# Attention scores on four quadrants of the matrix array, one chunk's router logits by VectorE, and a new step order, in a fused attention, MLP and routed-expert kernel

## The chip, the cores and the metric

The kernel runs on one core of one Trainium2 chip. The metric is the device time of one execution in microseconds (us). A core has five engines with a queue each: TensorE (PE: matmuls, and PEld: the weight loads before them), VectorE (DVE), ScalarE (ACT), GpSimd (POOL) and SyncE (SP, which issues most DMAs). Matmuls write PSUM; the other engines read it and work in SBUF.

## What is computed

Three layers follow each other; `x` goes from one to the next.

```python
# 1: attention of 2 batches x 8 heads x 768 positions, head_dim 64
k_sum = k.reshape(B, H, nb, 32, D).max(axis=3)       # 24 blocks a head
v_sum = v.reshape(B, H, nb, 32, D).mean(axis=3)
scores_l = where(|i - j| < 16, q @ k.T / 8, -1e9)    # a narrow window
scores_s = q @ k_sum.T / 8 + log(32)                 # and every block
a = softmax(concat(scores_l, scores_s)); out = a @ concat(v, v_sum)
# 2: x of 1536 tokens x 512
h = x @ w_in                                         # 512 x 2048
x = (h * sigmoid(h)) @ w_out                         # 2048 x 512
# 3: the best of 8 experts for each token
e = argmax(x @ w_gate)                               # 512 x 8
out = gate * (relu(x @ w1[e]) @ w2[e])               # 512 x 1024, 1024 x 512
```

## The kernel before

**Chunks.** The 1536 tokens are 6 chunks of 256 (`CH`), three to a batch; a chunk is 4 query tiles of 64 (`G`, `QT`). Heads go in pairs (`HP` = 4), 64 rows of head dimension each, so that a pair fills 128 partitions. A query tile needs 96 window keys and the 24 block keys: 120 columns (`NC`).

**Attention of a chunk and a head pair** is a row of steps, each one function: `D` (`dots`, line 318, scores on PE), `T` (`lows`, mask and maximum on DVE), `E` (`exps`, ACT), `R` (`shares`, DVE), `N` (`norm`, DVE), `P` (`turn`, four transposes on PE), `C` (`keep`, a copy out of PSUM), `V` (`values`, line 378, PE), `H` and `L` (`x_high`, `x_rest`: the result split in a high and a low part for ACT and DVE). `q` loads: for chunks 0 and 1 the queries alone, later also windowed keys and values. The keys of chunks 0 and 1 are cut from whole key tiles (`k`, loaded; `K`, block maxima on DVE; `W`, `windows`, POOL). The host lays the queries of a pair out as a block diagonal: the tile has 128 rows (two heads) and 128 columns (64 queries of one head, 64 of the other), with zeros in the two other blocks. One fp32 product of 128x128 with 120 moving columns so gives the scores of both heads, and a step has four such products into one PSUM tile (pool `ps_x` for chunks 0 and 1, `ps_a` later).

**The MLP** runs on split operands (a high part and a rest, three products for each). `F` (line 403, 24 products of N=256, the first four blocks in parts F0 to F3) makes 256 columns of h for a chunk in one of two PSUM tiles of pool `ps_h`; `t` (tanh, ACT), `u` (gating, DVE, the last reader of h), `g` and `w` split the result; `G` (line 440, 12 products of N=512) adds it into the chunk's two `ps_x` tiles. Its weights arrive packed (`l`), and steps `a`, `b`, `c`, `h`, `p` on ACT and DVE unpack and split them during the first 120 us. `x` copies a finished chunk out.

**The router** has two ways. `d` (`route_dots`, line 475): 16 products of a row tile with a broadcast column of `w_gate`, summed by DVE. Or, for the chunks named in `TURNED`, (4, 5) here: `rt` (line 486, four transposes on PE a tile), `rc` (a copy), `rl` (line 498, products with the gate on PE). `i`, `r` and `e` pick the expert, rank the tokens and write the table. After chunk 4 an early plan (`plan`, `prow`) chooses the first two expert units; `read`, `ids` and `ga` gather their tokens, `f1` and `f2` fetch their weights at an address from a register that the plan writes, `1h`, `1r`, `2h`, `2r` split those, `lt` turns the tokens. Then `f` (line 825 or 819) and `z` (line 866 or 860) are the experts' two layers, `ym` and `yo` scale and write.

**The order** of all this work is one list, `STEPS`: each word calls the next instance of one step, and each engine's queue has its instructions in that order. A mark says which engine takes a copy (' DVE, * ACT, _ POOL).

Of the kernel before, what the change touches and what calls it, by code (L numbers as in the profile page):

```python
# [58 lines left out]
C0* C0* D1 D1 D1 T1 E1 T1 T1 E1 P0 q1 C0* v0 b V0 H0 l l v0 R1 R1 L0 c v1 E1 N1 A0_ a V0 H0 R1 v0 A0_ N1 N1 V0 L0 H0 L0 h* a p h* b D1 b p P1 C1* l a A1_ l P1 P1 C1*  # L59
C1* l c F0 A0_ v0 V0 v1 v1 c h* V1 F0 F0 T1 h' H0 L0 F0 p b p F1 E1 F1 R1 c A1_ A1_ H1 L1 a b t u V1 v1 a l H1 V1 F1 H1 a N1 A1_ F2 q2 q2 A2_ F1 t l L1 P1 C1* L1 F2  # L60
F2 l l l l A2_ l V1 c b b a u c D2 T2 h* h* H1 L1 p b c p F3 F3 F3 g* w g* w F3 D2 h* p F2 c E2 a b h* p c t u l a t u h* h* p p a a b b c c g* g* G G l l a a a F t
F t w G w R2 N2 P2 h* h* b b c l h* c h* b p p p u u p b G C2* V2 a F c g* w l l F X q2 a c b b T2 c l l h* h* g* w c p t E2 G G h* h' u p p p F t H2 u g' a a b w a
l b a c t R2 N2 h* l c h* L2 G A2* p l P2 l b c b u l D2 T2 g* w F p c C2* V2 E2 h* p G h' p q2 A2_ F g* w G a b a b a a c c t h' h* b b D2 u g* l l l l c F h* w G l
p p p t c h' p a a t u u g' b b c w c F g* F H2 L2 T2 h* h* p p a E2 j G R2 N2 P2 w b c G t C2* q3 V2 u h' p R2 N2 P2 g* a w G q3 b c h' p F F t H2 u g' w L2 j G a a
b c h' p t j b u g' t u j C2' c h' p V2 H2 m m m m w L2 J B3' F F F t u g* g' J J w D3 t u T3 B3* J E3 G G R3 w D3 G t s g' w s N3 P3 u x* G g* s T3 C3' F E3 R3 N3
P3 w O d0 q3 s t u B3_ q3 Y M A3* G q4 A3' V3 F d0 d0 d0 C3* V3 g' w d0 t d0 d0 d0 B3_ u H3 G L3 H3 L3 D3 D3 T3 E3 T3 E3 d0 g' w F t F R3 R3 N3 N3 d0 u g* w P3 C3' t
u q4 g* B4_ D4 G A3* V3 H3 P3 A3' C3* T4 F E4 G d0 d0 d0 R4 N4 L3 t u g' d0 d0 d0 V3 H3 L3 F B4_ i r e e t F t w w u g' u w D4 T4 E4 x' d1 d1 d1 G F t q4 d1 d1 d1
B4_ P4 D4 T4 E4 q4 R4 A4* C4' G G V4 N4 P4 C4' R4 u d1 d1 d1 d1 g' F g* B4_ N4 t F w w t u g' u g' H4 L4 w D4 T4 E4 G G P4 C4* A4_ V4 d1 H4 F t R4 d1 q5 d1 d1 A4_ V4
H4 N4 L4 u g* d1 F B5' D5 G A5' w d1 q5 x* B5_ L4 T5 E5 i P4 C4' D5 T5 E5 d2 A4_ w F V4 H4 R5 R5 d2 L4 G N5 P5 t u d2 d2 d2 g* w d2 t u g* F r q5 N5 d2 d2 t u d2 d2
d2 w d2 d2 G G g* F t u g' F w d2 t u d2 d2 B5' C5' q5 G x* g' F F t t i V5 H5 d3 d3 w w d3 d3 d3 d3 d3 d3 L5 P5 G G u g' u D5 C5' T5 E5 F R5 e e A5_ V5 d3 d3 N5 g'  # L70
# [24 lines left out]
def fused_kernel(ctx: ExitStack, tc, qw, kw, kt, vw, vr, vt, w_in, w_out, w_gate, w1, w2, masks, blocks, items, out):  # L95
# [180 lines left out]
    qs, ks, vs, ws, dot = {}, {}, {}, {}, {}  # L276
# [790 lines left out]
```

## Time and profile before

| | before |
|---|---|
| median of 3 runs | 541.26 us (540.97 to 544.36) |
| the profiled execution | 540.3 us |
| its span, first to last instruction | 538.4 us |
| PE, DVE, ACT, POOL busy | 520.3, 427.4, 227.6, 81.5 us |
| moved by DMA | 76.25 MB |

The profile is one execution. The span leaves out 1.9 us around the instructions. An engine's busy time is the union of its instructions; matmuls are pipelined, so that what one costs is read from the distance between starts, or from a run of them on the chain that ended last, and not from its duration. A transfer costs when someone waits for it.

### The profile page before, as it was taken

What the parts mean: (1) busy time and instruction counts of PE and PEld (TensorE: products, weight loads), DVE (VectorE), ACT (ScalarE), POOL (GpSimd) and SP (SyncE); (2) the same over time, 40 slices, a digit from 0 to 9 for tenths busy, and PEclk for the clock granted to TensorE, in tenths of its full rate; (3) what the DMA queues carried; (4) which work ended last, traced back from release to release, by engine and by line L of the source; (5) the groups of instructions that cost most, each with busy time, mean ns of one, the idle gap of its engine ahead of it and who ended that gap; (6) DMA issues with size and microseconds to landing.
All of it is one profiled execution on the core that took longest, in us unless ns stands there. A gap on an engine that the chain in (4) does not pass through costs nothing.

```text
span 538.4 us, 9847 instructions
## 1 busy us (share of the span) xinstructions
PE 520.3 (97%) x3602; PEld 458.7 (85%) x3602; DVE 427.4 (79%) x1114; ACT 227.6 (42%) x546; POOL 81.5 (15%) x113
## 2 busy tenths in 40 slices
PE   7779999999999999999999999999999999999993
PEld 4579888989889898898988989898989889988882
DVE  4899999997778797788886364968769786879991
ACT  3799987652324332341122312242423422344551
POOL 3711000100000021001010323010334210220041
PEclk9999999999999999999999999999999999999997
DMA  8998545326573311420200208300264750347950
GB/s 326 367 311 304 178 158 167 97 84 211 175 243 97 92 54 54 126 73 5 88 16 1 40 1 313 110 9 1 62 241 141 265 196 0 106 163 266 326 187 15
DMA packets 40936, 76.25 MB, mean 142 GB/s; under 512 B 3910, under 2 KB 14764, under 8 KB 40882
## 3 DMA queue, kind: packets, MB, share of 16 engines
q1 hardware_dynamic: 35954, 65.83, 36.3%
q0 software_dynamic: 2912, 6.33, 3.3%
q10 hardware_dynamic: 2016, 3.40, 2.0%
q8 instruction: 30, 0.49, 0.4%
q14 instruction: 24, 0.20, 0.1%
HBM read 82.51 MB, written 7.19 MB: 167 GB/s over the span
## 4 chain that ended last, share of the span: by engine, by line
PE 79%; issue 11%; DVE 3%; ACT 2%; POOL 2%; DMA 1%; POOLq 0%; DVEq 0%; ACTq 0%
PE x L440 25%; PE h L403 25%; PE jh L825 11%; PE jy L866 9%; PE s L326 3%; PE o L384 2%; POOL out L875 2%; PE t L366 2%; ACT a L351 1%; PE xp L793 1%; DMA kt<-kt 1%; PE lo L504 1%; DVE dull L481 0%; DVE a L360 0%; DVE ksum L184 0%
## 5 line engine op out<-in xcount | busy, mean ns | idle before, releaser
L403 PE MATMUL h<-x,wi 128*128 128x256 f32 x1152 | 144.7, 282 | 0.0
L440 PE MATMUL x<-wo,g 128*128 128x512 f32 x576 | 142.5, 399 | 0.1
L403 PEld LDWEIGHTS h<-x,wi 128*128 128x128 f32 x1152 | 139.0, 188 | 1.8 <-DVE wi L270 0.2
L440 PEld LDWEIGHTS x<-wo,g 128*128 128x128 f32 x576 | 105.5, 188 | 23.5 <-DVE g L424 0.4
L786 DVE TENSOR_TENSOR sp<-r,sp 128x512 fp32r<-128x512 f32 x144 | 92.0, 683 | 7.7 <-ACT sp L164 7.3
L825 PE MATMUL jh<-xTT,sp 128*128 128x256 f32 x576 | 73.7, 284 | 0.0
L825 PEld LDWEIGHTS jh<-xTT,sp 128*128 128x128 f32 x576 | 71.6, 191 | 1.5
L866 PE MATMUL jy<-sp,jT 128*128 128x512 f32 x288 | 70.8, 397 | 0.0
L866 PEld LDWEIGHTS jy<-sp,jT 128*128 128x128 f32 x288 | 52.8, 188 | 11.4
L164 ACT CAST sp<-r 128x512 fp32r<-128x512 f32 x74 | 42.6, 620 | 42.3 <-DMA r<-w 30.1
L413 ACT ACTIVATE t<-h 128x512 f32<-128x512 f32 x48 | 28.5, 596 | 61.7 <-PE h L403 34.2
L351 ACT ACTIVATE a<-a,m 128x120 f32<-128x120 f32 x96 | 36.7, 384 | 36.0 <-DVE m L345 35.9
L416 DVE SCALAR_TENSOR_TENSOR t<-t,h 128x512 f32<-128x512 f32 x48 | 32.6, 682 | 16.4 <-ACT t L413 16.0
L481 DVE CUSTOM_DVE_ANT_0 dull<-row,gate 128x512 bf16<-128x512 f32 x64 | 44.1, 690 | 1.3
L834 ACT ACTIVATE jT<-jh 128x512 fp32r<-128x512 f32 x24 | 14.4, 598 | 58.9 <-PE jh L825 42.0
L424 DVE TENSOR_TENSOR g<-t,g 128x512 fp32r<-128x512 f32 x48 | 32.9, 695 | 3.5 <-ACT g L164 3.2
L164 DVE CAST sp<-r 128x512 fp32r<-128x512 f32 x70 | 28.3, 424 | 8.7 <-PE jh L825 6.4
L875 POOL DMA_INDIRECT out<-y,ids x15 | 21.3, 1419 | 74.3 <-ACT y L871 50.4
L164 POOL COPY k<-ksum 128x96 f32<-128x96 f32 x11 | 4.0, 363 | 176.2 <-DMA k<-kw 166.7
L345 DVE CUSTOM_DVE_ANT_0 a<-s,mask 128x120 f32<-128x120 f32 x96 | 21.2, 277 | 10.6 <-PE s L326 9.3
L164 ACT CAST g<-t 128x512 fp32r<-128x512 f32 x27 | 16.6, 622 | 26.6 <-DVE t L416 26.2
L552 POOL DMA_INDIRECT tbl<-tb,ix x12 | 12.7, 1056 | 63.1 <-DVE cum L544 60.8
(185 smaller groups left out, 618.9 us busy)
## 6 DMA issues: line engine op xcount, KB each, us to landing
r<-w SPq DMA_DIRECT2D x36, 1024.0 KB, 5.6
rawi<-w_in SPq DMA_DIRECT2D x16, 512.0 KB, 5.5
rawo<-w_out SPq DMA_DIRECT2D x16, 512.0 KB, 7.8
q<-qw SPq DMA_DIRECT2D x24, 256.0 KB, 6.9
v<-vw SPq DMA_DIRECT2D x24, 192.0 KB, 3.9
k<-kw SPq DMA_DIRECT2D x16, 240.0 KB, 3.5
kt<-kt SPq DMA_DIRECT2D x8, 416.0 KB, 4.9
x2d<-row ACTq DMA_DIRECT2D x12, 256.0 KB, 2.0
```

The costliest lines, as they stand in the source:

```text
L164: (nc.scalar.copy if by is nc.scalar else by.tensor_copy)(dst, src)
L351: nc.scalar.activation(a[:, t], a[:, t], AF.Exp, bias=m[:, 0, t:t + 1], scale=-1.0, accum_out=m[:, 1, t:t + 1])
L403: nc.tensor.matmul(hs[c, p][:, j], wi[p][:, u, k, j * P:(j + 1) * P], xt[c, k][:, v], start=(j + k + n == 0), stop=(j == 1 and k == KB - 1 ...
L413: nc.scalar.activation(t, hs[c, p], AF.Tanh, scale=0.5)
L416: nc.vector.scalar_tensor_tensor(ts[c, p], ts[c, p], 1.0, hs.pop((c, p)), op0=ALU.add, op1=ALU.mult)
L424: by.tensor_tensor(g[:, 1], ts.pop((c, p)), g[:, 0].bitcast(F32), op=ALU.subtract)
L440: nc.tensor.matmul(x2p[c][i], g[:, v, j, i * P:(i + 1) * P], wo[f][:, u], start=(f == 0 and n == 0), stop=(f == FB - 1 and n == 2))
L481: nc.vector.tensor_tensor_reduce(dull, r, gates[e], 1.0, 0.0, ALU.mult, ALU.add, lg[:, i * E + e:i * E + e + 1])
L786: by.tensor_tensor(dst[:, 1], src, dst[:, 0].bitcast(F32), op=ALU.subtract)
L825: nc.tensor.matmul(hps[i, p][:, j], sp1[p // 2 * 4 + k][:, u, f:f + P], x[v][:, k], start=(k + n == 0), stop=(k == 3 and n == 2))
L866: nc.tensor.matmul(yps[i, t], h[:, v, j, t * P:(t + 1) * P], sp2[2 * p + j][:, u], start=(p + j + n == 0), stop=(p == 3 and j == 1 and n = ...
L875: nc.gpsimd.indirect_dma_start(out=outs[j][:, :], out_offset=bass.IndirectOffsetOnAxis(ap=ids[:, j:j + 1], axis=0), in_=ys.pop((i, t)), in ...
```

## The change

1. The queries are no longer padded: the tile `q` of a chunk and pair is 128 rows (two heads) by 4 x 64 queries, half as many bytes (the host's `qw` is a plain transpose).
2. `dots` makes eight products a step, each of 64 rows (one head) and 64 columns (one query tile), that go in turn to the four quadrants of the array: row half by head, column half by the parity of the query tile. The two heads' scores go to two PSUM tiles: both of `ps_x` for chunks 0 and 1, one of `ps_a` and one of `ps_h` for the others. The later steps are as many as before; they take the tiles by the new places (`lows` with masks whose first and last variants differ between the partition halves, `values` with other slices).
3. `TURNED` is (5,): chunk 4 has 16 `d` steps in place of two each of `rt`, `rc`, `rl`, and its ranks go to a PSUM tile of their own.
4. `STEPS` is a new list: 1681 words in place of 1671. Apart from chunk 4's logits every step is there as often as before; some copies go to another engine.

```diff
-TURNED = (4, 5)
+TURNED = (5,)
 STEPS = """
-k K W1 k K q0 q0 W0 W0 D0 D0 T0 n Z E0 k k q0 T0 E0 R0 N0 P0 K K W0 D0 T0 E0 q0 W0 D0 T0 n W1 n W1 W1 R0 R0 E0 N0 Z Z C0* l l a R0 N0 N0 P0 a M A0_ q1 q1 q1 P0 b c
...
-l b a c t R2 N2 h* l c h* L2 G A2* p l P2 l b c b u l D2 T2 g* w F p c C2* V2 E2 h* p G h' p q2 A2_ F g* w G a b a b a a c c t h' h* b b D2 u g* l l l l c F h* w G l
...
-w w d3 d3 t d3 u F d3 B5_ A5' d3 d3 H5 L5 P5 C5* g' w G G V5 H5 r G t u g* i w D5 T5 E5 R5 G r N5 F t u g* P5 G C5' w G A5_ V5 H5 L5 L5 F F t x* u tiles g* w e rt rt
-F e e rc* rl rc' rl t u g* w t G u g* i w e r e F plan prow f2 F e f1 t t u G G g' w u g' read ids w ga ga 2h' 2h' 2r 1h* F t u G g* 2h* 2h' F t u g* lt w lc' w 1r
-1h' 1r F t u G G 2r 2r 2r g' f2 f2 f1 2h' lt w 1h* 2h' 2h' ls lc' G G 2r x* rt 1r 1h' ls f 1r f 2r 2r rt rc* rc* 1h* f1 1h' 1h* 1h' f f rh f f f ga ga 1r 1r 1r rl lt
...
+k K W0 W1 k k k q0 D0 K q0 W0 D0 q0 n K K W0 D0 W0 T0 T0 T0 Z E0 q0 W1 R0 D0 T0 E0 E0 E0 n n Z R0 R0 l a Z l a q2 N0 P0 C0* q1 q1 q1 q1 v0 N0 v0 N0 P0 C0* M W1 W1
+A0_ A0_ b A2_ R0 c h* D1 T1 D1 E1 l v1 v0 A0_ V0 H0 A0_ V0 T1 N0 l l l H0 v0 l E1 L0 L0 D1 P0 C0* V0 a b P0 C0* p H0 R1 R1 a c N1 b v1 P1 C1* A1_ l A1_ N1 h* T1 D1
...
+G D5 e T5 A5* G F F F t N5 t u u g' g' w E5 t L5 R5 N5 P5 P5 t G u d3 g' C5* V5 H5 d3 d3 w G C5' A5* V5 L5 u g' H5 L5 d3 d3 d3 d3 i w w F t F u t u g' G r w G x* F
+d4 d4 e d4 d4 d4 F F t t u d4 g* w G G g' w G t t d4 d4 d4 e e d4 u u d4 d4 d4 d4 d4 d4 i r e e F g* w g* w plan prow F G G t u tiles t read g' ids w F t u g* u w g* w
+G f1 G 1h* 1r 1h* 1h* 1h' f1 1h' ga ga lt 1h* lt G 1r 1r ga 1r 1r lc* ls lc' ls f2 f 2h' 2h* 2h* x* rt 2r 2r 2r 2h* 2r 1r 1h' 1r f2 f2 rc* 2h* 2h* rt rc* f f f f f f
...
 """
...
-            qs[c, hp] = q[:, hp]
+            qs[c, hp] = q[:, hp].rearrange("p a b -> p (a b)")[:, :CH].rearrange("p (g q) -> p g q", g=G)
+            rr[c, hp] = q[:NC, hp]
...
-        qs[c, hp] = at.tile([P, G, P], F32, tag="q", name=f"q{c}{hp}")
+        qs[c, hp] = at.tile([P, G, QT], F32, tag="q", name=f"q{c}{hp}")
...
-        pool, tag = (ps_x, "x2") if c < 2 else (ps_a, "a")
-        ps = dot[c, hp] = pool.tile([P, G, P], F32, tag=tag, name=f"s{c}{hp}")
-        if (c, hp) in ks:
-            k = ks.pop((c, hp))
-            for t in range(G):
-                nc.tensor.matmul(ps[:, t, :NC], q[:, t], k[:, t], start=True, stop=True)
-            return
...
+        pools = [(ps_x, "x2")] * 2 if c < 2 else [(ps_a, "a"), (ps_h, "h")]
+        dot[c, hp] = [pool.tile([P, 2, CH], F32, tag=tag, name=f"s{c}{hp}{h}") for h, (pool, tag) in enumerate(pools)]
+        k = ks.pop((c, hp), None)
+        for t in range(0, G, 2):
+            for h in range(2):
+                d = slice(h * D, (h + 1) * D)
+                for i in range(2):
+                    ps = dot[c, hp][h][i * QT:(i + 1) * QT, t // 2]
+                    o = (G * g + t + i) * QT
+                    if k is not None:
+                        nc.tensor.matmul(ps[:, :NC], q[d, t + i], k[d, t + i], start=True, stop=True)
+                        continue
...
-        for t in range(G):
-            n = G * g + t
-            v = 0 if n == 0 else 2 if n == S // QT - 1 else 1
-            nc.vector.tensor_tensor_reduce(a[:, t], ps[:, t, :NC], mask[:, v], -0.125, 3.0e38, ALU.add, ALU.min, m[:, 0, t:t + 1])
+        for j in range(G):
+            n = G * g + 2 * (j % 2)
+            v = 0 if n == 0 else 2 if n == S // QT - 2 else 1
+            nc.vector.tensor_tensor_reduce(a[:, j], ps[j // 2][:, j % 2, :NC], mask[:, v], -0.125, 3.0e38, ALU.add, ALU.min, m[:, 0, j:j + 1])
...
-            for i in range(0, P, D):
-                nc.tensor.matmul(ps[i:i + D, t], v[:, t, i:i + D], r[:, t, i:i + D], start=True, stop=True)
+            for h in range(2):
+                d = slice(h * D, (h + 1) * D)
+                nc.tensor.matmul(ps[d, t], v[:, t, d], r[:, 2 * h + t // 2, t % 2 * QT:(t % 2 + 1) * QT], start=True, stop=True)
...
-    qw = np.zeros((B, 3, HP, 2, D, G, 2, QT), q.dtype)
-    for i in range(2):
-        qw[:, :, :, i, :, :, i, :] = qh[:, :, i].transpose(0, 2, 1, 5, 3, 4)
+    qw = con(qh.transpose(0, 3, 1, 2, 6, 4, 5))
```

## Rows read from the trace of the kernel before

**Rows 1.** The page: engines' busy time; TensorE's granted clock in 40 slices.
```profile
PE 520.3 (97%) x3602; PEld 458.7 (85%) x3602; DVE 427.4 (79%) x1114; ACT 227.6 (42%) x546; POOL 81.5 (15%) x113
...
PEclk9999999999999999999999999999999999999997
```

**Rows 2.** Busy time by stretch: us, engines' busy us, PEclk, DMA share, GB/s.
```profile
20.00:50.00 30.00, 24.70 (x291) 23.19 (x292) 28.79 (x88) 28.36 (x83) 8.72 (x12) 1.00 1.04 337
50.00:120.00 70.00, 70.00 (x477) 61.95 (x477) 68.85 (x141) 54.10 (x114) 1.89 (x3) 1.00 0.42 137
120.00:300.00 180.00, 179.92 (x1345) 160.53 (x1344) 140.38 (x439) 54.89 (x166) 13.53 (x22) 1.00 0.29 93
...
300.00:350.00 50.00, 50.00 (x335) 44.99 (x335) 32.51 (x95) 12.91 (x23) 10.30 (x11) 1.00 0.38 125
350.00:530.00 180.00, 179.49 (x1100) 158.79 (x1098) 146.10 (x305) 68.08 (x126) 38.30 (x29) 1.00 0.42 148
```

**Rows 3.** Waits of PE: total us, times, longest; first and last of 8.
```profile
PE s L326 <- POOL a L164: 1.9, 2, 1.4
...
PE t L366 <- ACT a L351: 0.5, 1, 0.5
```

**Rows 4.** The chain that ended last: start us, us, what; D and V steps.
```profile
33.55 0.71 PE h L403 x6
...
39.46 1.08 PE o L384 x32
...
86.49 0.89 PE s L326 x8
87.38 2.83 PE h L403 x24
90.21 0.61 PE o L384 x16
90.83 3.00 PE x L440 x12
...
96.65 2.80 PE x L440 x12
```

**Rows 5.** Timeline of PE, start-up: fp32 products of N=512 in two runs.
```profile
10.39 1.88 PE L199 MATMUL vm<-vn,odds 128*120 128x512 f32 x4
...
15.71 3.60 PE L199 MATMUL vm<-vn,odds 128*120 128x512 f32 x8
```

**Rows 6.** DMA issues: count, KB each, median us to landing.
```profile
q<-qw SPq DMA_DIRECT2D x24, 256.0 KB, 6.9
```

**Rows 7.** Groups by line: busy us, mean ns, idle before; h's and s's readers.
```profile
L416 DVE SCALAR_TENSOR_TENSOR t<-t,h 128x512 f32<-128x512 f32 x48 | 32.6, 682 | 16.4 <-ACT t L413 16.0
L413 ACT ACTIVATE t<-h 128x512 f32<-128x512 f32 x48 | 28.5, 596 | 61.7 <-PE h L403 34.2 <-DVE g L424 19.8 <-PE cnt L566 5.4
...
L345 DVE CUSTOM_DVE_ANT_0 a<-s,mask 128x120 f32<-128x120 f32 x96 | 21.2, 277 | 10.6 <-PE s L326 9.3 <-PE t L366 1.1
```

**Rows 8.** The chain: chunk 4's transposes and logits on PE.
```profile
304.34 0.87 PE xr L491 x8
...
308.04 1.68 PE lo L504 x16
```

**Rows 9.** The chain: two logits of chunk 3 by DVE.
```profile
209.28 0.69 DVE dull L481
210.01 0.69 DVE dull L481
```

**Rows 10.** Timeline and chain, from the early plan to the first expert product.
```profile
321.07 0.17 DVE L607 CAST regs<-fresh 128x2 int32<-128x2 f32 x1
...
322.57 0.39 SPq L762 DMA_DIRECT2D r<-w  x1
...
331.41 0.62 ACT L164 CAST sp<-r 128x512 fp32r<-128x512 f32 x1 [12.14 <-DMA r<-w]
...
348.56 1.43 PE jh L825 x12
```

More of the change, by code (lines that the diff above doesn't have):

```diff
@@ L65 @@
[L65 to L68, printed above, removed]
@@ new lines @@
+u L2 g' V2 w l a F b c h' p H2 L2 m t u q3 F F F t s u g* g* j G w j J J w t G B3* D3 t G X m s u g' u g' j J j x* w J T3 w G m s m s E3 R3 N3 F t B3* Y M O q3 u g*
+d0 d0 F d0 B3_ A3_ A3_ P3 D3 T3 d0 t d0 G q3 C3* V3 D3 H3 u T3 F w E3 R3 N3 P3 F g* C3* d0 d0 q4 L3 t u d0 E3 R3 g* V3 H3 B3_ N3 D3 T3 t A3_ L3 G d0 w d0 P3 E3 d0 G
+w C3* V3 H3 R3 N3 d0 d0 d0 d0 L3 F t P3 u d0 u q4 g' w G A3_ i C3* V3 H3 x* B4_ D4 T4 q4 B4_ B4_ d1 E4 L3 F t d1 g* D4 T4 u R4 N4 G P4 g* w w E4 d1 r F F t e u g*
+A4_ d1 d1 d1 d1 d1 d1 C4* V4 t u g' H4 L4 D4 d1 G G w F t F T4 E4 A4' A4_ R4 N4 P4 q4 B4* d1 u w d1 d1 g' w d1 R4 t u g' G C4* V4 D4 T4 q5 d1 d1 E4 i F t u F x* G q5
@@ new lines @@
+N4 P4 C4* g* R4 N4 d2 d2 d2 d2 w w H4 L4 G B5* D5 d2 d2 d2 T5 G V4 d2 d2 F E5 R5 N5 A4_ P4 C4' t t H4 L4 u u g* G B5_ V4 H4 L4 r F P5 w q5 d2 t u g* C5' w g* w d2
+B5_ d2 d2 A5* A5* F t u g* d2 d2 d2 i D5 T5 E5 G G G e e x' w R5 N5 D5 T5 d3 d3 d3 d3 F E5 q5 P5 F V5 t u t H5 L5 u d3 g' w g' G C5* w V5 H5 B5_ e r d3 R5 d3 F d3 d3
+G D5 e T5 A5* G F F F t N5 t u u g' g' w E5 t L5 R5 N5 P5 P5 t G u d3 g' C5* V5 H5 d3 d3 w G C5' A5* V5 L5 u g' H5 L5 d3 d3 d3 d3 i w w F t F u t u g' G r w G x* F
+d4 d4 e d4 d4 d4 F F t u d4 g* w G G g' w G t t d4 d4 d4 e e d4 u u d4 d4 d4 d4 d4 d4 i r e e F g* w g* w plan prow F G G t u tiles t read g' ids w F t u g* u w g* w
@@ L86 @@
+z z 2r 2r 2h* 2h' 2h* 2h* 2r 2r f2 1r rh z 2h' z ht ht f1 1r f f f 1r f f hc' yo rr yo 2r 2r 2r f z z hc' rr 2h' 2h' 2r 2r f2 rh 2h* ht hc* 2r z 2h' 2r z z z z z ym*
+yo ym* yo rr z z z 2h' 1h* 1h* 1h' 1h' 1h* 2r 1r 1r f 2h* 1r f f 2h* rh 1r f ht 1r f 2r 2r 1r f z hc' rr z 2h* f2 rh ht 2r z 2h' z 2r hc* 2h' 2r 2h* 2h* 2h* rr z 2r
+2r ym' 2r z z z z yo ym* yo
 """
@@ L274, in fused_kernel @@
     xt = {}
-    qs, ks, vs, ws, dot = {}, {}, {}, {}, {}
+    qs, ks, vs, ws, rr, dot = {}, {}, {}, {}, {}, {}
     def rooms(c):
@@ L320, in dots @@
         q = qs[c, hp]
-        pool, tag = (ps_x, "x2") if c < 2 else (ps_a, "a")
-        ps = dot[c, hp] = pool.tile([P, G, P], F32, tag=tag, name=f"s{c}{hp}")
-        if (c, hp) in ks:
-            k = ks.pop((c, hp))
-            for t in range(G):
-                nc.tensor.matmul(ps[:, t, :NC], q[:, t], k[:, t], start=True, stop=True)
-            return
-        for t in range(G):
-            o = (G * g + t) * QT
-            nc.tensor.matmul(ps[:, t, :KW], q[:, t], kts[b, hp][:, o:o + KW], start=True, stop=True)
-        for t in range(G):
-            nc.tensor.matmul(ps[:, t, KW:NC], q[:, t], ksum[:, b, hp], start=True, stop=True)
+        pools = [(ps_x, "x2")] * 2 if c < 2 else [(ps_a, "a"), (ps_h, "h")]
[10 more added lines that the diff above has]
+                        continue
+                    nc.tensor.matmul(ps[:, :KW], q[d, t + i], kts[b, hp][d, o:o + KW], start=True, stop=True)
+                    nc.tensor.matmul(ps[:, KW:NC], q[d, t + i], ksum[d, b, hp], start=True, stop=True)
     def lows(c, hp):
@@ L341, in lows @@
         m = at.tile([P, 3, G], F32, tag="m", name=f"m{c}{hp}", bufs=4)
-        for t in range(G):
-            n = G * g + t
-            v = 0 if n == 0 else 2 if n == S // QT - 1 else 1
-            nc.vector.tensor_tensor_reduce(a[:, t], ps[:, t, :NC], mask[:, v], -0.125, 3.0e38, ALU.add, ALU.min, m[:, 0, t:t + 1])
+        for j in range(G):
+            n = G * g + 2 * (j % 2)
+            v = 0 if n == 0 else 2 if n == S // QT - 2 else 1
+            nc.vector.tensor_tensor_reduce(a[:, j], ps[j // 2][:, j % 2, :NC], mask[:, v], -0.125, 3.0e38, ALU.add, ALU.min, m[:, 0, j:j + 1])
         att[c, hp] = (a, m)
@@ L371, in keep @@
         if c < 2:
-            r = qs[c, hp][:NC]
+            r = rr[c, hp]
         else:
@@ L1020, in _arrays @@
     near = np.abs(i + WINDOW - w) < WINDOW
-    for n, ok in enumerate((near & (w >= WINDOW), near, near & (w < KW - WINDOW))):
+    first, last = near & (w >= WINDOW), near & (w < KW - WINDOW)
+    odd = np.arange(P)[:, None] >= QT
+    for n, ok in enumerate((np.where(odd, near, first), near, np.where(odd, last, near))):
         masks[:, n, :KW] = np.where(ok, 0.0, 8 * NEG)
```

36 lines of the change are left out of this document (16 added, 20 removed).

## The prediction

> **What bounds the kernel now.** I read the page first: TensorE (PE) is busy 97% of the span and its granted clock is 1.00 in all slices but the last [rows 1], so no term below is about the clock. Then the windows: from 50 to 530 us PE is busy without a break, while VectorE (DVE) is busy 68.85 of the 70 us from 50 to 120 us, 140.4 of 180 us up to 300 us, 32.5 of 50 us up to 350 us and 146.1 of 180 us after that [rows 2]. PE's own waits are eight small groups, 9.2 us in all, the largest 1.9 us [rows 3], and all but a trace of them lie before the first h block at 33.55 us [rows 4]. So a microsecond of PE work that is taken away after 120 us is a microsecond of time; one taken away before 34 us is none by itself, since PE waits there for others; and one taken away between 34 and 120 us is worth something only if DVE, which is full, doesn't become the one that ends last. The sum is made against the profiled execution: 538.4 us of span, 540.3 us in all, 0.96 us under the median of 541.26.
>
> **Scores as quadrants.** A D step goes from 4 products of 128 rows, 128 columns and N=120 to 8 products of 64 rows, 64 columns and N=120. In the profile each fp32 product is two instructions, so 8 become 16. Before: 0.89 us a step, with no loss for the matmul behind it (2.83 us of h as elsewhere) [rows 4]. The trace has no 64x64 product; the nearest row is the V step (values), 8 products of 120 rows and 64 columns that go in turn to two halves of the columns, N=64. Two facts come from it. First, concurrency: two V steps back to back take 1.08 us and one takes 0.61, so a V step behind another costs 0.47 us for 16 instructions, or 0.059 us a pair [rows 4]. How fast one instruction streams is shown by the N=512 fp32 products: four instructions more make 3.60 out of 1.88 us, 0.43 us each, 0.84 ns a column [rows 5], so N=64 takes 0.054 us. A pair takes as long as one: the two column halves run fully side by side. Second, a change of array shape costs something: a lone V step takes 0.61 - 0.47 = 0.14 us on entry, and the x block behind it 3.00 in place of 2.80 us, 0.20 us on leaving [rows 4]. Together 0.34 us.
> The rule that the Trainium skill has for this (TensorEngine Tiling, Key Properties) is that a change of tiling mode drains TensorE; the trace agrees, with those 0.34 us. The same page (Key Properties) lets the four 64x64 tiles run in parallel, which no row here shows; by it alone the gain would be the 0.46 us below.
> For a quadrant step, N=120 streams in 120 x 0.84 = 0.101 us. If all four quadrants run side by side there are 16/4 = 4 rounds: 0.40 us, with some start cost between instructions (a pair's 0.059 against 0.054) 0.42 to 0.44. With 0.34 for the shape it is 0.77 us against 0.89: a gain of 0.12 us a step. The ends: if the shape change costs nothing, 0.43 us, a gain of 0.46; if only two quadrants run side by side, as the V row shows and no more, 8 rounds, 0.86 + 0.34 = 1.20 us, a loss of 0.31. I take 0.12, because the V row shows both facts on the same engine, and the two heads write different banks. In the new list nearly every D stands alone between full-array work, so almost none shares a shape change. Of 24 D steps, 8 (chunks 0 and 1) lie in the start-up, where PE waits: no credit. 16 x 0.12 = **1.9 us**; the 4 of chunk 2 fall into the stretch with a full DVE, so I count 12 to 16 of them and take **1.6 us**.
>
> **The padding that goes.** Each q transfer falls from 256 to 128 KB [rows 6], 24 of them, 3 MB. Behind 120 us the queues have air and this is worth nothing. From 20 to 50 us the DMA engines are busy throughout [rows 2]; 8 transfers of 128 KB less at 340 GB/s are 3 us of that traffic. But ScalarE and DVE are equally full from 20 to 50 us (28.4 and 28.8 of 30 us), so I credit 0, with 3 us as the far end.
>
> **The second PSUM tile of a D step.** For chunks 2 to 5 it now takes one of two ps_h buffers, which the F blocks alternate between. A later F, and everything behind it on PE, then waits until T (DVE) has read the scores, and a D waits until tanh and the gating have read an earlier F. Followed through the new list, the tightest places have one whole F or G block (2.8 us) between the end of the old user and the start of the new. The need is 0.60 (tanh) + 0.68 (gating) or 4 x 0.28 (T) [rows 7] and some tenths for signals: below 2 us. I take 0; a DVE queue that runs 1 us late would cost up to 1 us at each of the 7 tightest places. For chunks 0 and 1 a step takes two ps_x buffers of four in place of one, so two steps are in flight, not four; that is in the start-up, where T at 1.1 us a step is followed by more DVE work anyway.
>
> **Chunk 4's logits.** Away go 8 transposes (0.87 us) and 8 fp32 products in 16 instructions (1.68 us) of PE, on the chain at 304 and 308 us [rows 8]: **2.55 us**, taken off a full engine, and two copies. 16 products by DVE come, one each 0.73 us by their starts [rows 9]: 11.7 us, in a stretch where DVE idles 17.5 of 50 us [rows 2]. That is the cover; behind them in DVE's queue stand the gating steps of chunk 5, the ranks of chunk 4 and the early plan, which fetches the first expert's weights. Before, that plan's registers are written at 321.07, the transfer that they release is issued at 322.57 and its first piece converted at 331.41; the first expert product starts at 348.56 [rows 10]. From the plan to the first product I need 10.3 us of fetch and 0.62 + 4 x 0.69 us of conversion, some 14 us. In the new list 7 F and G blocks stand between the plan and the first expert product, 19.7 us (11 blocks before, 31 us). So 6 us are left as cover: 0 taken, and one for one beyond that. After 350 us DVE has 34 us of air for the weight conversions that are put off.
>
> **The new order.** Counting steps, the first F parts come with about the same work of PE, DVE and ScalarE ahead of them as before, and the nine first whole F blocks with the same DVE work. I take 0, within 3 us either way: PE's 9 us of waits before 34 us are what a better start could win, and a start in which all four k tiles go ahead of the first q puts the first D later by about two transfers. The tail is the same: a scale, one indirect write.
>
> Sum: 1.6 + 2.55 = 4.1 us. 540.3 - 4.1 = 536.2, and with the 0.96 us to the median **537.1 us**, 0.8% below.
>
> **Rivals.**
> (a) *Shape changes are nearly free and the start gains.* For it: the V row may owe its 0.34 us to its own weight loads. Gain 16 x 0.4 + 2.55 = 9 us, with up to 3 us from the start: 529 to 532. Against it: two places in the trace show the 0.34.
> (b) *Quadrants in pairs only; slower.* The place is PE's queue: two instructions of one product use the same quadrant, and if the second holds the queue until the first is through, at most two quadrants are busy. A D step is then 1.20 us, +0.31; the 16 steps lose 5.0 us and the early 8 up to 2.5; less 2.55 that is +2.4 to +5: 543.7 to 546.2. It turns the sum from 0.89 + 2.55/16 = 1.05 us a step on. Against it: V's pairs would be slowed by the same cause and are not.
> The Trainium skill (TensorE: Matmul & The Clock Gate, Part 3) holds that matmuls start and end strictly in program order, which is the rule that would bring this about; V's 0.059 us a pair speaks against its biting here, unless the instructions are issued in another order than written.
> (c) *The plan comes late.* 11.7 us of DVE work stand ahead of it, where transposes and products took 5.4 us from start to end [rows 8]; past the 6 us of cover each us is lost. With the DVE 10 us late, +4, net 0: 541.
> (d) *The start is worse* by 2 to 4 us (late first D, DVE as the bound up to 120 us): 539 to 541.
>
> **Chances.** Forecast (533.5 to 538.5) 0.44; (a) 0.23; (b) 0.13; (c) 0.08; (d) 0.12. A range of 531 to 544 leaves out the better half of (a) and the worse half of (b) and little else. About 1% (5.4 us) is what a measurement of this kernel can tell from no change: below 535.85 lie (a) and a quarter of the forecast, 0.34; above 546.7 some of (b) and of worse cases, 0.07; the rest, 0.59, between.
>
> **What would show it.** D steps on the chain at 0.43 us with 0.2 us on the block behind (right), at 0.86 us (b), or with nothing behind (a). No xr and lo pieces between 300 and 320 us, and no wait of PE for DVE's gating or the ranks there. The first expert product about 4 us earlier than 348.6 us with no wait before it; a wait there for the transfer or for sp's conversion is (c). The first h block before or after 33.55 us, with more or less than 9.2 us of PE waits, is (d). The prediction is wrong if PE shows new waits past 120 us, or if the start moves by more than 3 us.

## The result, and the profile after

| | before | after |
|---|---|---|
| median | 542.0 us (540.97 to 544.36, 4 runs) | 548.78 us (547.88 to 550.21, 4 runs) |
| ratio after/before, 95% interval | | 1.0142 [1.0108, 1.0177] |
| span of the profiled execution | 538.4 us | 547.1 us |

Slower by 1.4% (the two medians alone give 1.0125), where 0.8% faster was forecast; 548.78 lies outside the forecast's range. The page of after, busy times and granted clock, against [rows 1]:

```profile
PE 523.3 (96%) x3770; PEld 450.9 (82%) x3770; DVE 435.0 (80%) x1136; ACT 229.2 (42%) x552; POOL 78.3 (14%) x115
...
PEclk9958999999999998999999999999999999999998
```

There are two dips of the clock that before has not: slices 3 and 4, and slice 16. The windows say the same against [rows 2] (PEclk is the third number from the end). The second fence is finer; the clock is 0.70 from 25 to 30 us and 0.59 from 40 to 45 us, so that the half clock stands from about 27 to 44 us:

```profile
20.00:50.00 30.00, 24.19 (x275) 20.42 (x274) 26.24 (x76) 23.39 (x68) 8.53 (x12) 0.72 0.98 301
...
120.00:300.00 180.00, 176.52 (x1423) 153.37 (x1421) 132.00 (x417) 64.47 (x191) 14.36 (x21) 0.99 0.28 89
300.00:350.00 50.00, 50.00 (x333) 43.97 (x332) 39.12 (x131) 11.64 (x22) 11.89 (x13) 1.00 0.22 82
350.00:530.00 180.00, 178.79 (x1104) 158.10 (x1102) 152.99 (x321) 62.45 (x116) 32.16 (x28) 1.00 0.45 158
```
```profile
30.00:35.00 5.00, 4.32 (x42) 3.05 (x40) 3.89 (x21) 4.57 (x15) 0.00 (x0) 0.50 1.06 292
35.00:40.00 5.00, 2.96 (x36) 2.44 (x35) 4.61 (x11) 3.66 (x14) 0.93 (x2) 0.50 1.10 346
...
208.00:211.00 3.00, 3.00 (x8) 2.33 (x9) 0.00 (x0) 0.00 (x0) 0.12 (x1) 0.50 0.56 145
```

PE's waits, against [rows 3]: the largest is new, and it is not in the start.

```profile
PE o L390 <- POOL v L165: 4.7, 2, 3.5
PE s L334 <- POOL a L165: 2.8, 1, 2.8
PE t L371 <- DVE x L398: 1.3, 1, 1.3
...
PE xr L497 <- ACT row L453: 0.8, 2, 0.4
```

Its place, in the timelines of PE and of POOL (start, us, engine, line, idle before and what ended it):

```profile
206.69 0.69 PE L390 MATMUL o<-r,v 120*64 120x64 f32 x16 [3.48 <-POOL v L165]
207.31 0.64 PE L334 MATMUL s<-k,q 64*64 64x120 f32 x16
```
```profile
199.90 1.17 POOL L558 DMA_INDIRECT tbl<-tb,ix  x1 [3.29 <-DVE cum L550]
206.03 0.61 POOL L165 COPY v<-vsum 24x512 f32<-24x512 f32 x1 [4.97 <-DMA tbl<-tb,ix]
```

The chain behind it shows both levels of the clock: the x blocks at 207.95 take 7.34 us, where two blocks otherwise take 2 x 2.80 (0.50 is 1.2 of 2.4 GHz). It also shows the quadrant step, 0.57 us, with 0.2 us on the block behind (2.99 for 2.80; at 241.45 an h block with 0.2 behind a V step, as in before [rows 4]):

```profile
207.38 0.57 PE s L334 x16
207.95 7.34 PE x L446 x24
...
234.46 2.81 PE x L446 x12
237.27 0.57 PE s L334 x16
237.84 2.99 PE x L446 x12
240.83 0.61 PE o L390 x16
241.45 3.03 PE h L409 x24
```

I lay the two traces side by side at four marks that both have: the start of the 193rd h product, of the first expert product, of the last one, and the end of the span.

| us | before | after | difference of the stretch |
|---|---|---|---|
| 193rd h product | 80.3 | 86.2 | +5.9 |
| first jh product | 348.3 | 353.6 | -0.6 |
| last iy product | 529.1 | 537.4 | +3.0 |
| end of the span | 538.4 | 547.1 | +0.4 |

The middle stretch holds 3.5 us of the wait at 203 us and 1.7 of the half clock behind it. Without them it is 5.8 us shorter, where 16 x 0.12 + 2.55 = 4.5 were worked out (experiment 2 shows where most of the rest comes from). So the two parts that I costed came in, and three losses that I put at nothing, the start (5.9), the wait (5.2) and the experts' part (3.0), ate them. Below, "the mark" is the start of the 193rd h product.

### The profile page after: what moved, and what is told of

Its sections match the earlier page's. It is cut to its first block, busy times and chain, and to the rows that moved or that the text cites. A ratio compares the mean times of both kernels' runs of the same rounds, so it can differ in the third digit from the quotient of the medians.

```text
span 547.1 us, 10244 instructions
## 1 busy us (share of the span) xinstructions
PE 523.3 (96%) x3770; PEld 450.9 (82%) x3770; DVE 435.0 (80%) x1136; ACT 229.2 (42%) x552; POOL 78.3 (14%) x115
## 4 chain that ended last, share of the span: by engine, by line
PE 49%; DVE 4%; issue 3%; DMA 3%; ACT 0%; POOL 0%; SPq 0%; POOLq 0%; ACTq 0%
PE jh L831 11%; PE x L446 11%; PE jy L872 10%; PE h L409 10%; DMA r<-w 2%; PE jh L825 2%; DVE sp L792 1%; PE iy L866 1%; PE xp L799 1%; PE o L390 1%; DMA ents<-tbl,rix 1%; PE s L334 1%; PE t L371 1%; POOL out L881 0%; PE hp L846 0%
## 5 line engine op out<-in xcount | busy, mean ns | idle before, releaser
L446 PEld LDWEIGHTS x<-wo,g 128*128 128x128 f32 x576 | 106.7, 190 | 25.3 <-issue 1.6
L487 DVE CUSTOM_DVE_ANT_0 dull<-row,gate 128x512 bf16<-128x512 f32 x80 | 55.1, 688 | 1.6
L165 ACT CAST sp<-r 128x512 fp32r<-128x512 f32 x70 | 39.9, 621 | 21.7 <-DMA r<-w 16.4
L165 DVE CAST sp<-r 128x512 fp32r<-128x512 f32 x74 | 30.3, 439 | 3.9 <-PE jh L831 2.0
L881 POOL DMA_INDIRECT out<-y,ids x15 | 17.5, 1164 | 111.1 <-ACT y L877 71.7
L855 DVE SCALAR_TENSOR_TENSOR jT<-jh,jT 128x512 fp32r<-128x512 f32 x24 | 16.5, 686 | 13.0 <-ACT jT L840 13.0
```

What stands on the lines that cost most here:

```text
L165: (nc.scalar.copy if by is nc.scalar else by.tensor_copy)(dst, src)
L446: nc.tensor.matmul(x2p[c][i], g[:, v, j, i * P:(i + 1) * P], wo[f][:, u], start=(f == 0 and n == 0), stop=(f == FB - 1 and n == 2))
L487: nc.vector.tensor_tensor_reduce(dull, r, gates[e], 1.0, 0.0, ALU.mult, ALU.add, lg[:, i * E + e:i * E + e + 1])
```

## Experiments

Each time is a median beside runs of the kernel before on the same chip (541.09 to 541.96 us), with the ratio to them.

**1. The wait at 203 us.** `e` issues chunk 0's table write on POOL's queue; `A4_` is POOL's copy of the block means into chunk 4's `v`.

```diff
-... E4 d1 r F F t e u g* A4_ d1 d1 ...
+... E4 d1 r F F t u g* A4_ e d1 d1 ...
```

> The changed kernel with one word of the list moved: chunk 0's first table write (e) stands behind the copy of chunk 4's means into v (A4_) on GpSimd's queue, not before it. If the wait of 3.6 us of a values step for that copy, and the 3.4 us of half clock behind it, are lost for good: 544 to 545 us, 4 us less, no wait at 203 us. If later slack on PE takes them back, or the wait is for something else: 548 to 549 us.

543.53 us, 1.0042 [1.0023, 1.006]: by the medians 5.25 us less than after, for one word; 4 us were forecast. I call it the mended kernel below. The same place in its chain has neither the wait nor the half clock (24 x products in 5.80 us, not 7.34):

```profile
203.17 0.61 PE o L390 x16
203.79 0.57 PE s L334 x16
204.36 5.80 PE x L446 x24
```

**2. The quadrants alone.** First, the new list with block diagonal queries and one PSUM tile a step (the code of before for them, chunk 4's logits still on VectorE).

```diff
-        pools = [(ps_x, "x2")] * 2 if c < 2 else [(ps_a, "a"), (ps_h, "h")]
+        pool, tag = (ps_x, "x2") if c < 2 else (ps_a, "a")
...
+                nc.tensor.matmul(ps[:, t, :NC], q[:, t], k[:, t], start=True, stop=True)
```

> The changed kernel's list and its chunk 4 logits by VectorE, but the scores by four padded 128x128 products and one PSUM tile as before, padded q transfers too. Theory A (the list is what costs, a quadrant step is 0.12 us cheaper than a padded one): slower than the changed kernel by 16 to 24 x 0.12 us, 1.9 to 2.9 us, near 551 us; D steps 0.89 us on the chain. Theory B (the quadrants are what costs: thin PE work in the start lets the clock fall, and scores hold ps_h): faster than the changed kernel by 5 us or more, 544 us or less, no half clock between 27 and 44 us.

552.07 us, 1.0205 [1.0176, 1.0234]: 0.63% above after, 3.4 us, which the two intervals hold to within 2.4 us. The wait at 203 us is there too, so it is not the quadrants'. In the traces the mark is at 86.4 us, as in after (86.2), so that the early steps show no gain; from there to the first jh product the quadrants save 2.6 us (270.0 against 267.4), with 14 steps. A step alone between full-array blocks gains 0.12 us (0.88 + 2.80 against 0.57 + 2.99). One right behind a V step gains more, since the padded step takes longer there; first the padded kernel, then after:

```profile
226.85 1.08 PE s L327 x8
227.94 5.66 PE h L404 x48
```
```profile
224.80 0.57 PE s L334 x16
225.37 5.85 PE h L409 x48
```

That is 0.32 us, and 5 of the 14 steps stand behind a V step: 9 x 0.12 + 5 x 0.32 = 2.7 us. Second, the list of before with quadrants in chunks 3 to 5 alone.

```diff
+        if c < 3:   # block diagonal, one PSUM tile; else quadrants, as in the change
```

> The kernel before with its own list and its logits on TensorE, and quadrants in chunks 3 to 5 alone (12 of 24 steps; chunks 0 to 2 keep the block diagonal). Theory A, a step's 0.12 us comes through in the old order too, and the second PSUM tile costs nothing there: 12 x 0.12 = 1.4 us less, 540 to 540.5 us. Theory B, the ps_h buffers that the steps now share with the F blocks cost TensorE waits in a list that was not made for it: 542 us or more, with waits of h products for DVE's a or of s products for DVE's t past 180 us.

547.77 us, 1.0126 [1.0101, 1.0152]: 6.4 us more. PE's waits from 100 to 345 us are all at the shared ps_h buffers: a D that waits until the gating `t` has read an earlier F, an F that waits for `lows` (the `m` of T):

```profile
PE s L340 <- DVE t L436: 2.8, 2, 2.3
PE h L423 <- DVE m L360: 1.8, 2, 1.1
```

They are 4.6 us in the trace, against 12 x 0.12 us gained; from the mark to the first jh product it takes 271.4 us in place of 268.0. The experts' part, which the edit doesn't touch, takes 183.1 us in place of 180.8. So in this list the second PSUM tile costs more than the quadrants gain; after has none of these waits.

**3. The start.** Extra bf16 products of N=512 (18 at the front in place of 10, and 18 in five places before P and V steps), whose results nobody reads, hold the clock up:

```diff
-        wake(10)
+        wake(18)
...
+ nc.tensor.matmul(ps, z[:, :P], z, ...)   # 3 or 4 at each new word wk3, wk4
```

> The changed kernel with more idle products for TensorE in the first 40 us: 18 for 10 at the beginning, and 3 or 4 ahead of five steps that waited there (N=512 bf16, 0.21 us each at full clock). If the half clock between 27 and 44 us is what costs: granted clock 1.00 from some 8 us on, first h block 2 to 4 us earlier, 544 to 546 us. If the waits for data set the start: the clock is full and the first h block no earlier than 38.5 us, 547.5 to 550 us.

547.24 us, 1.0104 [1.0078, 1.0131]: by the medians 1.5 us less than after, which the intervals don't tell from nothing. The clock is at 1.00 from 30 to 45 us and the first h product comes at 36.20 in place of 39.49, as the first theory has it, but a V step then waits for its values, and the mark is at 86.5 us, no earlier:

```profile
44.98 0.69 PE L396 MATMUL o<-q,v 120*64 120x64 f32 x16 [4.09 <-DMA v<-vw]
```

The value loads alone, in the mended kernel: the last two v1 loads exchanged with chunk 2's second load `q2` (three transfers) that stands ahead of them.

```diff
-... V0 P1 L0 E1 T1 q2 E1 l l l ... h* C1* v1 v1 F2 C1* ...
+... V0 P1 L0 E1 T1 v1 v1 E1 l l l ... h* C1* q2 F2 C1* ...
```

> The kernel with e behind (543.5 us), and one exchange in the list: the last two v loads of chunk 1 change places with the second load step of chunk 2, some 40 words earlier. If these loads, which landed at 43 us here and at 35 us before the change, set the start: blocks from the second F on 3 to 5 us earlier, 538.5 to 541 us. If the clock or another chain sets it: 542.5 to 544 us.

544.29 us, 1.006 [1.0034, 1.0086]: nothing against 543.53, with the mark at 84.9 us. Both remedies together:

> The same with the idle products of the warm run. If half clock costs once the loads are early: 2 to 4 us under the run without them. If it doesn't: within 1 us of that run.

541.28 us, 1.0007 [0.9974, 1.004]: 2.3 us under the mended kernel by the medians, the mark at 81.4 us. In the traces each of the two loses what the other leaves late. Next, the old order of the start: the old list's first 121 words (up to its first F0), then the rest of the new list.

```diff
-k K W0 W1 k k k q0 D0 K q0 W0 D0 q0 n K ...
+k K W1 k K q0 q0 W0 W0 D0 D0 T0 n Z E0 k ... (121 words), then what is left of the new list
```

> The changed kernel with the first 121 words of the old list (up to the first F part) ahead of the rest of the new list. If the new start is what costs: first h block at 33 to 34 us, no half clock after 20 us, 541.5 to 543.5 us. If the start's gain is given back because VectorE is full up to 120 us in either order: 546 us or more.

547.04 us, 1.0112 [1.0082, 1.0141] (this kernel still has the wait at 203 us), the clock at 0.50 again from 35 to 40 us, the first h product at 37.3 and the mark at 83.5. With these 121 words, the extra products and `e` behind `A4_`, but without the exchange of the v1 loads:

> All three remedies on one kernel with quadrants: the old list's first 121 words, the extra products that hold TensorE's clock, and `e` behind `A4_`. The extra products are work that the result does not need. Theory A, the loss lies in three separate places (start order, clock in the start, the table write ahead of the means): 547.04 of the old start less 5.25 for `e` less 1.5 to 3 for the clock, 539 to 540.5 us, with clock 1.0 from about 25 us on and the last iy product 3 to 5 us earlier than in the version with new start, warm clock and early v loads only if the start was its bound. Theory B, the start's remedies all end at one bound (VectorE full from 40 to 120 us), so that the old start gives nothing on top of the warm clock: 541 to 542.5 us, first x as before or earlier but h384 no earlier than 131.8 us.

541.95 us, 1.0018 [0.9985, 1.0051]: theory B, nothing on top of the warm clock. Is it the quadrants, shorter steps with two ps_x buffers each? The next kernel has block diagonal queries in chunks 0 and 1, the old 121 words, `e` behind `A4_` and no extra products.

```diff
+        if c < 2:
+            ps = dot[c, hp] = ps_x.tile([P, G, P], F32, tag="x2", ...)   # as before
```

> Quadrants for chunks 2 to 5 only: chunks 0 and 1 keep the block diagonal queries, one PSUM tile a step and the old list's first 121 words; then the new list with `e` behind `A4_`; chunk 4's logits by VectorE; no extra products. Theory A, in the start it is the quadrants themselves that cost (a step that is shorter and holds two ps_x buffers leaves TensorE longer pauses, in which its clock falls): the first h block at 33 to 34 us, clock 1.0 from about 10 us on as before, and 547.04 of the old start with quadrants less 5.25 for `e` less 3 to 4: 537.5 to 539 us. Theory B, the old start with the new rest is late for other reasons (loads that the new list asks for at other times): first h at 36 us or later, half clock again before 42 us, 541 us or more.

543.79 us, 1.0045 [1.0025, 1.0065]: the first h product at 37.4 us without quadrants too, so theory A falls. Its timeline shows what stands there:

```profile
31.69 0.65 PE L383 MATMUL t<-ident,a 128*120 128x128 f32 x4 [1.39 <-ACT q L165]
34.18 1.15 PE L403 MATMUL o<-q,v 120*64 120x64 f32 x32 [1.84 <-POOL v L165]
36.31 1.12 PE L403 MATMUL o<-q,v 120*64 120x64 f32 x16 [0.98 <-POOL v L165]
37.37 3.30 PE L422 MATMUL h<-x,wi 128*128 128x256 f32 x18
```

V steps that wait for POOL's copies stand in PE's queue ahead of the first F part, whose operands are there. Counted in the lists: ahead of the first F0 word 6 V steps in the new list (and in the old 121 words with the new rest), 3 in the old. So I took the old list's first 188 words, up to chunk 2's first D, in which F parts and V steps alternate.

```diff
-... V0 P1 V1 V1 F0 F0 F0 P1 P1 F0 F2 V1 F2 V1 F1 ...      (new list, its D, P, V, F words)
+... P1 P1 F0 V0 V1 F0 F0 F0 F1 F1 V1 V1 F1 F2 F1 P1 ...   (old words up to 188)
```

> As the kernel with block diagonal queries in chunks 0 and 1 and the old list's first 121 words (543.79 us), but with the old list's first 188 words, so that the first parts of F stand between the V steps as before (3 V steps ahead of the first h block in place of 6). Theory A, the start's loss is that the new list puts V steps, which wait for POOL's copies of the means and for the value loads, ahead of the first F parts in TensorE's queue: first h at 33.3 us as before, h192 near 80 us, and 543.79 less 3 to 4: 540 to 541 us. Theory B, the four us come from what is in the queues before word 121: no change, 543 to 544.5 us.

> The same 188 old words with quadrants in chunks 0 and 1 as well. Theory A1, quadrants do no harm in the start: the same as with block diagonal queries there within 1 us, first h at 33 to 34 us. Theory A2, they do (two PSUM buffers a step, or a fallen clock): first h at 35 us or later with the clock at half for some us, and 1.5 to 4 us more than with block diagonal queries in chunks 0 and 1.

542.18 us, 1.0001 [0.9966, 1.0036], and with quadrants everywhere 540.44, 0.9973 [0.9947, 0.9998]. The first h product is at 33.5 and 31.7 us. With quadrants:

```profile
31.66 1.63 PE L409 MATMUL h<-x,wi 128*128 128x256 f32 x6
33.22 1.63 PE L390 MATMUL o<-q,v 120*64 120x64 f32 x32
34.78 1.45 PE L409 MATMUL h<-x,wi 128*128 128x256 f32 x10
```

The V steps behind the first F part find their values and wait no more (the clock is 0.66 from 30 to 35 us). The mark is at 80.8 us (86.2 in the mended kernel, the same but for the start): 5.4 us in the trace, 3.1 in the medians. The block diagonal version has it at 83.2 us, hardly earlier than with 121 words (83.4). Both versions have two waits of 0.7 us of h for x at 45 to 47 us, but only there the clock falls behind them (0.80 from 45 to 50 us), and an x block takes 4.49 us in place of 2.96. The third kernel of 5 has that same start, and its mark is at 81.0 us. So A1 holds, and the 1.7 us between the two medians, whose intervals overlap, show no gain of the quadrants.

What the V steps alone cost is not shown by this. The kernel with early loads and extra products keeps the 6 of them and has the mark at 81.4 us. And the first kernel of 4 has the mended kernel's start word for word, but in its trace the clock was low for a shorter time:

```profile
30.00:35.00 5.00, 3.22 (x56) 2.39 (x56) 4.97 (x25) 5.00 (x20) 0.00 (x0) 1.00 1.05 309
35.00:40.00 5.00, 4.02 (x33) 3.93 (x34) 4.96 (x11) 4.67 (x12) 0.99 (x2) 0.66 1.09 354
```

Its mark is at 83.1 us, some 3 us earlier than the mended kernel's. One start differs by that much between two traces, and the half clock differs with it.

**4. Chunk 4's logits.** The mended kernel, but the logits on TensorE, `rt`, `rc` and `rl` in the places of the `d4` words.

```diff
-d4 d4 e d4 d4 d4 F F t u d4 g* w G G g' w G t t d4 d4 d4 e e d4 u u d4 d4 d4 d4 d4 d4 i r ...
+rt e rt rc* F F t u g* w G G g' w G t t rc' rl rl e e u u i r ...
```

> The kernel with e behind (543.5 us), chunk 4's logits by PE again at the places of the d4 words. If those 16 steps cost nothing in the new list: 2.5 us more, 546 us. If they make the plan and the first experts' weights late by the 2 us that PE loses between 340 and 400 us: 543.5 to 544.5 us, and those waits gone.

547.06 us, 1.0113 [1.008, 1.0146], 3.5 us above the mended kernel, 1 us more than the first theory. In the traces the stretch from the mark to the first jh product grows from 262.2 to 267.8 us, 5.6 us: 2.55 of PE's work, a wait of 1.10 at the ranks and 1.74 of half clock in the h block behind it. The last two belong to my placing:

```profile
324.81 0.17 PE L534 MATMUL lo<-oh,tri 128*128 128x8 bf16 x1 [1.10 <-DVE oh L528]
...
324.94 4.57 PE L409 MATMUL h<-x,wi 128*128 128x256 f32 x24
```

In the old list with the code of before, 16 `d4` between chunk 4's rows and its ranks:

```diff
-tiles g* w e rt rt F e e rc* rl rc' rl t u g* w t G u g* i w e r e F
+tiles g* w e d4 d4 d4 d4 F e e d4 d4 d4 t u g* w t d4 d4 d4 G u g* w d4 d4 d4 d4 d4 d4 i e r e F
```

> The kernel before, its list and padded scores, with chunk 4's logits by VectorE alone: 16 d4 in place of rt, rc and rl between chunk 4's rows and its pick. If they are worth what PE no longer does: 2.5 us under the kernel before, 538.5 to 539.5 us. If the early plan comes too late for the first expert product: 541 us or more, with a wait of PE ahead of that product.

554.4 us, 1.0236 [1.0196, 1.0276]. PE has the ranks in its queue, and DVE comes to them only after the 16 products:

```profile
PE rk L529 <- DVE oh L523: 11.9, 1, 11.9
```

So I put the ranks, the plan and all that hangs on it four F and G blocks later, and, as the control, did the same with the logits on TensorE:

```diff
-r e F plan prow f2 F e f1 t t u G G g' w u g' read ids w ga ga 2h' ...
+F F t t u G G r e g' w u g' w F plan prow f2 t u G e f1 g* F t u g* w w F read ids ga ga 2h' ...
```

> The kernel before (padded queries, its own list) with chunk 4's logits by VectorE, as in the earlier trial in the old list, but with the ranks, the table, the early plan and all that follows from it put four F and G blocks later against the MLP's words. Theory A, the step is worth its 2.55 us as soon as the ranks have room: 538 to 539.5 us and no wait of PE for DVE's oh tile over 1 us. Theory B, the 11.7 us of VectorE work are owed somewhere in any case and the plan's delay only moves them to the first expert products: 541 to 545 us with a wait of jh products for ACT or DVE tiles between 340 and 360 us.

> The kernel before (block diagonal queries, logits of chunk 4 on TensorE, its own list), with only the ranks, the early plan and what follows from it four F and G blocks later, so that the plan stands some 16 us ahead of the first expert product in place of 27. Theory A, the experts' part loses its 3 us in all kernels with the new list because the plan, and with it the fetch of the weights, stands only 15 us ahead of the first product there: first to last expert product 183 to 184 us in place of 180.8, and 543.5 to 545 us. Theory B, the distance has cover and the 3 us belong to the rest of that part's order: 180.8 us and 541.5 to 542 us.

553.1 us, 1.0222 [1.0148, 1.0296], and 554.22, 1.0225 [1.0195, 1.0255]. Side by side they say that my new place for the plan costs some 13 us by itself, more than either theory gave it, and that the logits' place makes no difference that these two can tell (1.1 us). In the control PE waits for `t` in the MLP and then for the turned tokens of the first unit (`xTT`), which now come too late, and its clock falls twice there and once more at 507 us:

```profile
334.92 4.59 PE L404 MATMUL h<-x,wi 128*128 128x256 f32 x24 [2.70 <-DVE t L417]
...
354.83 0.63 PE L492 MATMUL xr<-ident,row 128*128 128x128 f32 x4 [2.71 <-DVE xTT L808]
...
357.47 2.71 PE L826 MATMUL jh<-xTT,sp 128*128 128x256 f32 x11 [1.76 <-DVE xTT L808]
```

**5. The experts' part.** The version of 3 with the warm clock and early loads (541.28 us) with the old list's order from the first expert block on; then the same with block diagonal queries in chunks 0 and 1 and the old 121 words, and with the old 188 words:

> The new list up to the first expert block (with `e` behind `A4_`, two v1 loads early and the extra products for the clock, 541.28 us when run with the new list's rest), then the old list's order of the remaining steps. Theory A, the 3.5 us that the version with the new rest loses from the first expert product to the last come from the new order of that part: 537.5 to 538.5 us, first to last product in about 181 us as before. Theory B, they come from what stands ahead (the plan comes later in the new list, weights and gathered rows arrive later): 540.5 to 542 us with the first to last product still about 184 us.

> As the kernel with block diagonal queries in chunks 0 and 1 and the old start, and from the first expert block on the old list's order as well. Theory A, the three losses of the new list are separate and all come back: the old expert order gives the 2 us that it gave in the version with the warm start, 535.5 to 537 us, 0.8 to 1% under the kernel before. Theory B, what is gained ahead of the experts is lost behind them (the weights that they wait for arrive no earlier): 538.5 us or more, first to last expert product 183 us or more.

> The first of these three with the old list's order from the first expert block on too. Theory A, that order is worth 2 us as it was in the version with the warm start: 538 to 539 us, first to last expert product in 182 us. Theory B, it is worth nothing (as in the kernel with the first 121 old words, where it gave 1.04 us more, not less): 540 to 541.5 us.

540.41 us, 0.9982 [0.9941, 1.0023]; 544.83, 1.006 [1.004, 1.008]; 541.22, 0.9988 [0.9952, 1.0025]. First to last expert product: 182.0, 183.2 and 184.1 us. The first took 2.3 us out of that stretch, but against their counterparts with the new order (541.28, 543.79, 542.18) the three are 0.9 us faster, 1.0 slower and 1.0 faster, none of it clear of the intervals. The first lies between its theories, the other two at theory B: that the order of this part is the cause is not shown.

## Why the prediction was wrong

**The step that failed is the term of the new order, "I take 0, within 3 us either way"**, and with it "no term below is about the clock". I compared the lists by counts of steps ahead of a point, not queue by queue. In its place the traces show three losses:

- The start: +5.9 us at the mark. PE is granted half its clock from 27 to 44 us, and with the clock held up it waits for value loads that land late; both remedies together take 4.8 us back. In PE's queue 6 V steps, which wait for POOL and ACT, stand ahead of the first F part, not 3. The old order of 188 words takes 5.4 us back, the old 121 words, with 6 V steps still ahead, 2.75. So that the start's order is the cause is shown, and that the half clock is a part of it; how much the V steps are stays open. Rival (d) had the place, 2 to 4 us and the late first D (8.5 us, 7.1 before), but DVE as its bound, which is idle more than before there (26.24 against 28.79 us busy).
- The wait at 203 us: +5.2 us. On POOL's queue `e` stands right in front of a copy of chunk 4's means. The prediction followed what stands on PE, DVE and ScalarE, and says nothing of POOL's queue. The copy waits for the landing of the transfer in front of it, V waits for the copy: 3.5 us, with the half clock 5.2, and one word moved back gives 5.25.
- The experts' part: +3.0 us, of which 1.2 are waits of PE. Its cause stays open (under chunk 4's logits).

**The quadrant step** was right: 0.57 + 0.20 = 0.77 us, worked out from the V row and the 0.34 us for the shape; (a) and (b) are refuted by the rows at 237 us. (The sign that I named, 0.43 us on the chain, left out the 0.14 us on entry.) The four quadrants side by side are shown as well, where two steps follow each other in the start of after:

```profile
21.75 1.05 PE L334 MATMUL s<-a,q 64*64 64x120 f32 x32
22.73 1.15 PE L390 MATMUL o<-q,v 120*64 120x64 f32 x32
```

The two take 0.98 us, so that the second adds 0.41, where 4 rounds of 0.101 us were worked out. What was wrong is "nearly every D stands alone": 5 of the 14 steps behind the mark stand behind a V step and gain 0.32 us, so that these 14 gave 2.6 us in the traces, where I took 1.6 for 12 to 16.
The rule of the Trainium skill on tiling modes (TensorEngine Tiling, Key Properties: a change of mode drains TensorE) agrees with the 0.20 us on the block behind. The Trainium skill's rule on program order (TensorE: Matmul & The Clock Gate, Part 3) doesn't bite here: 16 instructions of N=120 in 0.57 us.

**The second PSUM tile**: 0 was right for the new list, which keeps a block between the users. The price that I named for a late DVE, "up to 1 us at each of the 7 tightest places", is of the kind that the old list pays (4.6 us at four places).

**The padding**: no gain that can be told apart. The new list with block diagonal queries has full clock from 15 to 39 us, but waits 4.1 us for a q load and 3.9 us for values, and comes to the mark at the same time as after.

**Chunk 4's logits**: -2.55 us in PE's work as worked out. The cover was thinner than the 6 us that I had left. From the plan's registers to the first expert product I counted 19.7 us; the trace has 15.0 (27.5 before [rows 10]), against a need of 14. I had counted the blocks behind the plan's word in the list. Its product on PE stands at 332.50, 21.1 us ahead of the first expert product, but the plan's own steps on DVE take 6.1 us before the registers are written:

```profile
332.50 0.05 PE cnt L572
...
338.60 0.08 DVE regs L611
...
340.74 12.69 DMA r<-w
...
353.98 0.62 ACT sp L165
354.60 0.50 ACT row L453
```

The need was met even so: the first expert product starts at 353.60 without a wait, and the first conversions of its weights at 346.32, 7.7 us behind the registers (10.3 before):

```profile
346.32 1.66 ACT L165 CAST sp<-r 128x512 fp32r<-128x512 f32 x3
```

The 12.69 us are a later transfer, of the second layer's weights. Its conversion stands ahead of chunk 5's row copies on ACT, so that PE waits for these (0.8 us), and later for the table's entries (0.4). Rival (c) named this place, but VectorE's 11.7 us are not the cause: with the logits on TensorE the distance is 15.9 us and the experts' part takes 183.1 us as well. Nor is the late plan shown to be it. The kernels in the old list with quadrants in chunks 3 to 5 and with 16 `d4` have the plan 27.4 and 28.2 us ahead, and the part takes 183.1 and 183.0 us there too, with waits late in it that before does not have; in the first of them:

```profile
PE hp L860 <- ACT hr L850: 0.9, 1, 0.9
PE jh L839 <- DVE sp L806: 0.7, 1, 0.7
```

The control in 4, with the plan 22 us ahead, has 189.2 us, but also some 10 us of half clock in that part. What makes the other 1.8 of the 3.0 us stays open.

With the start's order and `e` mended, the change is 0.3% faster than before (540.44 us, with an interval that all but touches 1). In its trace it is 4.0 us ahead at the first expert product (344.3 against 348.3), and the experts' part gives 4.2 back (185.0 against 180.8 us), 2.3 of it in the same two waits.

## What to carry to other kernels

Read a new order queue by queue: for each engine, what stands ahead of work that is ready (here F parts behind V steps on PE, which may be a part of the loss), and what a moved step is put in front of on the queue that issues its DMA (here a table write in front of a copy that PE needs). Count a plan's distance from the instruction that writes its result, not from its word in the list. Before a difference of 3 us in one stretch gets a cause, look at a second trace of the same stretch. A saving of a tenth of a microsecond a step can be worked out to the digit from the nearest rows and still be lost to one word of the list. A shared buffer is free only in the order that was made for it: a part of a change tried in the old order has a price that belongs to neither.

## What was not expected of the hardware

- A pause of PE can cost more than itself. After 3.48 us of waiting the clock stood at 0.50 from 208 to 211 us, and two x blocks took 7.34 us in place of 5.6; 1.10 us of waiting at the ranks was followed by an h block of 4.57 us in place of 2.83. It need not: two pauses of 0.9 and 0.7 us in the experts' part of the kernel with 547.77 us had a clock of 1.00 behind them.
- In the start the granted clock was 0.50 from 30 to 40 us with PE busy 4.32 and 2.96 of 5 us; with the extra N=512 products between the steps it was 1.00 there. Before, it was 1.00 from 25 to 35 us, with PE busy 2.72 and 2.87 of 5 us.
- A POOL copy behind an indirect write waited 4.97 us for that write to land. With `e` behind the copy, the next copy on POOL has an idle time of 5.44 us in front of it, and nobody waits for it. The wait is for a semaphore that the program names; whether the engine would wait without one is not shown.
